# Loading the front of a fused state-space and MLP kernel in fewer, longer transfers

## The chip, the core and the metric

The kernel runs on one core of one Trainium2 chip. The metric is the device time of one execution in microseconds (us), as the median of several executions. Five engines run their own instruction lists in order and wait for each other through semaphores: PE (matrix multiply), DVE (vector), ACT (scalar functions), POOL (general) and SP, which in this kernel does nothing but issue DMA transfers between memory (HBM) and the on-chip buffer (SBUF), or from one place of SBUF to another.

## What is computed

The sequence has S = 2048 rows and D = 512 channels, in bf16. Part A is a state-space mixer, part B a sequence-mixing MLP; both sit on a residual stream.

```
def _A_ref(q, k, v, shift_k, ssm_k, ssm_D):      # q is layernormed
    k_shift = sum over t<4 of k_pad[:, t:t+S] * shift_k[:, 3-t]
    kv = k_shift * v
    y = causal convolution of kv with ssm_k, by FFT of length 2*S
    y = y + kv * ssm_D
    return q * y
def _B_ref(x, w1, w2, w3, w4):
    h = _gelu(_layernorm(x) @ w1)                # then shifts by 1 or 2 rows per quarter
    x1 = x + hs                                  # hs = shifted h @ w2
    return x1 + _gelu(_layernorm(x1) @ w3) @ w4
x = A_q
h = x + _A_ref(_layernorm(x), A_k, A_v, A_shift_k, A_ssm_k, A_ssm_D)
out = h + _B_ref(_layernorm(h), B_w1, B_w2, B_w3, B_w4)
```

## The kernel before, in words

Row s of the sequence is written s = 32 n + 16 h + t, with n < 64, h < 2 and t < 16. The long convolution is a Fourier transform of 64 x 32 points, done as matrix products.

**The order is written out by hand.** The function does not issue instructions directly. Every step is registered with `add` (lines 87 to 105) as a numbered operation with the engines that may do it, a planned cost, what it reads and what it writes. `plan.issue()` then walks the text `ISSUE` (lines 40 to 72): a list of operation numbers, each with a letter (A, V, G) where the engine is a choice. So each engine's program is the order of this list. The planned costs decide nothing at run time.

**Transfers.** All of them go out from SP, in the order of the list, through `dma` (line 218). In the front they are these. `load_k`, `load_v`, `load_h` (lines 221 to 231) bring k, v and the long filter `ssm_k` in twelve transfers of 512 KB, each to all 128 partitions. Line 233 brings the 512 x 4 taps of the short filter into `ssk_bf` in pieces of 8 bytes, line 239 the 512 values of `ssm_D` into `dcol` in pieces of 2 bytes. `k_rows` (lines 426 to 433) moves the product kv from its row layout (`kvqt`, two buffers) to the layout that the transform wants (`Rk`): 16 transfers of 128 KB, each from every second partition and for 256 of the 512 channels, in pieces of 512 bytes. Lines 511 to 514 load the first EARLY = 8 of the 16 rows per partition of q into the place of k once k has been read (two transfers of 512 KB, each to 64 partitions). Lines 366 to 371 spread a table into `Wc` in four transfers. Lines 547 to 549 load all of q into `q_sb`, as two transfers of 1 MB to 64 partitions each, and lines 532 to 539 move four pieces of a second table (`Wf2`).

```
        for h in range(2):
            for g in range(2):
                dma(0.5, lambda h=h, g=g: nc.sync.dma_start(
                    Rk()[g * N1:(g + 1) * N1, 16 * h + 4 * qr:16 * h + 4 * qr + 4, :],
                    kvqt[qr % 2][h:P:2, :, g * 256:(g + 1) * 256]),
```

**The compute of the front.** `k_transposed` (line 383) turns k on PE, four rows at a time (`pk`), and ACT copies the result to `kta`. `k_taps` (line 406) applies the short filter as 32 products per half group with the diagonal matrices `dg` (`psh`, line 417) and DVE multiplies by v into `kvq` (line 422). `dg` is built by DVE at line 299 from the identity matrix and the taps. `h_layout` (line 436) turns the long filter on PE after POOL has added `ssm_D` to its first column (line 517). Stage A (`stage_a`, line 453) is 32 groups of products, 16 of k (`pak`) and 16 of the filter (`pah`); ACT or DVE converts each into `Tk` or `Th` (lines 161 and 163). `Th` lies where the tables lay that `Wc` is filled from, so its conversions wait for those transfers. Stage C (`stage_c`, line 478) multiplies `Th` and `Tk` with `Wc` (`pch`, `pck`), the results are converted to `xt`, and `product` (line 601) multiplies the two spectra on DVE (lines 616 to 623). The mean and variance of every row of q are taken on DVE (`stats`, line 575, operations `bst` at line 576 and `mvq` at line 577): rows 0 to 7 from the early copy, rows 8 to 15 from `q_sb`. These have their places in DVE's list too, among the conversions and products. After that follow the inverse transform, the gate with normalized q, and part B, which keeps PE busy to the end.

Of the kernel before, what the change touches and what calls it, by code (L numbers as in the profile page):

```python
# [16 lines left out]
P = 128  # L17
# [23 lines left out]
23 2 20 4 0 8 1 3 5 21 6 33 10 37 7 13 27 24 12 28 25 9 82 11 30 18 83A 17 92 69 43 26 80 120 93A 14 15 31G 22  # L41
102 32 94 81A 41 71G 96 72 58 42 95 45 103A 86 97 127 46V 59 84 63 61 121 60 47 100 64 98 130 36 87 19 101 53G
99 62 112 54 16 44 85 55 56 122 131A 39 89 123 219 91 40 213 88 90 223 34 128 124A 220 207 35 209 38 104 224 57
211 129A 29 113 49 67 65 125 225 66 48 68 70 50G 105 114 203 126A 210 51 212 73G 106 214 221 52 115 183 132 226
74 119 179 107 75 177 76 111 185 78 170 184A 180V 110 117 178A 199 77 116 186V 175 108 200A 193 118 176V 197
194A 109 191 204 192V 198A 205 173 195 174A 208 79 189 206 196V 154 190A 156 155V 142 157A 152 222 153V 166 229
143A 217 164 215 227 228 165V 167A 140 138 141V 139A 171 181 172A 182V 144 187 145A 188V 201 150 202A 256 160
151V 146 161A 168 147V 162 169A 148 249 158 163A 263 255 159V 149A 261 237 264A 257 243 259 133 262A 258V 134
271 260A 137 273 135 245 272A 136 269 265 274A 275 266 270A 281 244 268 276A 287 267 285 282A 246 278 283 288A
277 284A 299 279 297 286A 280 300A 293 290 295 298A 289 311 296A 216 294V 305 312A 307 218 291 306A 309 292 302  # L50
321 310A 323 301 308A 317 322A 303 304 324A 329 313 319 318A 314 331 320A 333 315 330A 316 335 250 334A 325 345
332A 326 336A 343 328 341 346A 327 247 347 418 342A 337 383 361 364 338 344A 363 231 365 348A 340 362 339 349
350 352 351 248 353 388 354 398 389A 355 356 386 399A 358 396 357 387A 390 366 360 359 397A 394 391V 368G 404
395A 369G 405V 406 384 407A 367G 385V 392 414 251 393A 253 230 415V 408 252 400 409A 372G 402 401V 410 403A 412
371G 411V 419 413A 373G 235 374A 416 460 254 381V 379G 233 468 461A 238 236 234 232 469A 462 420 463 370A 428
470 421A 466 417 471 500 239 464 240 472 429A 241 474 242 501A 508 422 473 475 376A 467 465 430 377A 423 548 431
375A 424 476 378A 477 426 509A 478 434 479 432 484A 540 427 502 485A 488 694 435 510 486A 433 489 425 511 487A
503 380A 491 436 512 438 549A 437 504 490 514 439 446A 447V 382G 505 506 444A 450 515 513 507 445A 516 492 518
451V 517 541A 519 448 524V 525A 542 528 498 449A 527V 550 529 493 454 543 499 520 546 458 455 531 551 526A 496
521 547 554 459 530 452 544 497 480 481 456 552 453 545 494 553 555 457 482 556 558 532 557 495 536 533 559 565V  # L60
589 564V 537 569 483 566V 567V 560 570 534 440 590 522 441 538 591 568 596 442 586 539 443 598 571 535 597 599
612 587 588 592 572 593 584 578 573 594 523 576 595 579 614 600 602 601 574 613 577 615 575 603 604V 607A 605V
606V 608 616 638 609A 617 580 624 610 641 581 611V 640 713 618 585 717 714 582 583 701 620 561 718 646 695 702
562 639 563 697 619 625 643 703 698 642 696 667 622 704 623 648 719 621 668 626 627 699 647 720 644 705 649 645
700 650 715 651 706 652 653 711 716 628 709 712 629 632V 707 654 710 655 660V 721 708 669 661 630A 664 636V 722
633 656A 724 666 634A 657 665 658V 637 674 670 671 662V 728 663 672 659 673 676 729 680 675 723 631 677 725 635
684 682 683 678 726 679 685 775 730 757 776 766 732 791 758 727 747 681 792 692V 690A 733 748 745 734 759 746
686A 739 760 687 737 740 735 738 691 741 736 753 693 742 755 754 731 749 756 751 750 743 752 793 744 789 794 783
790 785 767 771 768 762 772 804 688A 786 689 761 784 770 769 811 763 795 812 765 787 796 781 788 779 782 773 780
797 774 777 798 835 778 823 836 821 813 805 814 822 824 817 806 819 818 799 807 829 820 808 842 809 764 830 831  # L70
810 825 832 815 826 827 833 800 834 828 816 838 801 802 837 803 847 839 840 841 843 848 849 850 844 846 845
# [50 lines left out]
def kernel(  # L122
# [48 lines left out]
    FUSED = ()  # L171
    EARLY = (8)
# [4 lines left out]
    slot("B", [P, 15360], "kta")  # L177
# [17 lines left out]
    def dg():  # L195
        return X["kta"][:, 9216:11264].rearrange("p (c j s) -> p c j s", c=DC, s=P)
# [16 lines left out]
    dcol = cst.tile([P, DC], BF16)  # L213
    ssk_bf = cst.tile([P, DC, 4], BF16)
# [6 lines left out]
    def load_k(r0):  # L221
        dma(1.4, lambda: nc.sync.dma_start(k_sb()[:, r0:r0 + 4, :], kd.rearrange("(p t) d -> p t d", t=NT)[:, r0:r0 + 4, :]),
            r=("C",), w=[("k", r) for r in range(r0, r0 + 4)])

    def load_v(qr):
        dma(1.4, lambda: nc.sync.dma_start(v_sb()[:, qr, :, :], vd[:, 4 * qr:4 * qr + 4, :]),
            r=("C",), w=[("v", qr)])

    def load_h(c):
        dma(1.4, lambda: nc.sync.dma_start(X["hraw"][:, c, :], A_ssm_k[c * P:(c + 1) * P, :]),  # L230
            r=("S1",), w=[("h", c)])

    dma(0.5, lambda: nc.sync.dma_start(ssk_bf[:], A_shift_k.rearrange("(c p) j -> p c j", p=P)), w=["sskb"])
# [5 lines left out]
    dma(0.5, lambda: nc.sync.dma_start(dcol[:], A_ssm_D.rearrange("(c p) -> p c", p=P)), w=["dcol"])  # L239
# [38 lines left out]
    add({"G": 0.6}, lambda: make_identity(nc, ident[:]), w=["id"])  # L278

# [6 lines left out]
    def numbers():  # L286
# [11 lines left out]
    add({"V": 1.1}, numbers, r=["pidx"], w=["pf"])  # L298
    v(2.3, lambda: V.tensor_tensor(
        out=dg().rearrange("p c j s -> p (c j) s"), in0=ident[:].unsqueeze(1).to_broadcast([P, 4 * DC, P]),  # L300
        in1=ssk_bf[:].rearrange("p c j -> p (c j)").unsqueeze(2).to_broadcast([P, 4 * DC, P]), op=MUL),
# [64 lines left out]
    for d in range(4):  # L366
        dma(1.5, lambda d=d: nc.sync.dma_start(
            X["Wc"][d:P:4, :, :, d].rearrange("p a b c d -> p (a b) (c d)"),
            X["tta"][d:P:4, 0:6144].rearrange("p (a x) -> p a x", a=48)),
            r=["A", "W"] + [("t", a, hf) for a in range(3) for hf in range(2)] + [("wz", a, e) for a in range(3) for e in range(4)],  # L370
            w=[("Wc", d)])
# [32 lines left out]
    kvqt = [cst.tile([P, 4, D], BF16, name=f"kvq{i}") for i in range(2)]  # L404

    def k_taps(qr, u):
# [3 lines left out]
        def pe():  # L410
            pv = psum("psb", key)[:].rearrange("p (t d) -> p t d", d=D)
            for i in range(2):
                for c in range(DC):
                    for j in range(4):
# [3 lines left out]
                                  rhs=dg()[:, c, j, :], start=(j == 0), stop=(j == 3))  # L418
# [4 lines left out]
            out=kvqt[qr % 2][:, 2 * u:2 * u + 2, :], in0=X[key][:].rearrange("p (t d) -> p t d", d=D),  # L423
            in1=v_sb()[:, qr, 2 * u:2 * u + 2, :], op=MUL), ["C", key, ("v", qr)], [("kvq", qr % 2, u)])

    def k_rows(qr):

        for h in range(2):
            for g in range(2):
                dma(0.5, lambda h=h, g=g: nc.sync.dma_start(  # L430
                    Rk()[g * N1:(g + 1) * N1, 16 * h + 4 * qr:16 * h + 4 * qr + 4, :],
                    kvqt[qr % 2][h:P:2, :, g * 256:(g + 1) * 256]),
                    r=["C", ("kvq", qr % 2, 0), ("kvq", qr % 2, 1)], w=[("Rk", qr, h, g)])
# [19 lines left out]
    def stage_a(w, i, ring):  # L453
# [14 lines left out]
        if w == "k":  # L468
            src = ["C"] + [("Rk", qr, h, g) for qr in range(4) for h in range(2) for g in range(2)]
        else:  # L470
            src = ["S2"] + [("Rh", cc, b) for cc in range(2) for b in range(2)]
# [6 lines left out]
    def stage_c(w, c, hf, ring):  # L478
# [17 lines left out]
        add({"A": 1.05, "V": 1.4},  # L496
# [13 lines left out]
    qd = A_q[0].rearrange("(n h t) d -> h n t d", h=2, t=NT)  # L510
    for h in range(2 if EARLY else 0):
        dma(0.3 * EARLY, lambda h=h: nc.sync.dma_start(
            k_sb()[h * N1:(h + 1) * N1, 0:EARLY, :], qd[h, :, 0:EARLY, :]),
            r=("C",), w=[("k", t) for t in range(EARLY)])

    for cc in range(2):
        add({"G": 0.3}, lambda cc=cc: G.tensor_tensor(out=X["hraw"][:, cc:DC:2, 0], in0=X["hraw"][:, cc:DC:2, 0],
                                                      in1=dcol[:, cc:DC:2], op=ADD),
            ["S1", "dcol"], [("h", cc), ("h", cc + 2)])
# [12 lines left out]
    for hf in range(2):  # L532
        for h in range(2):
# [4 lines left out]
            dma(0.4, rows, wfs + [("kvq", 1, 0), ("kvq", 1, 1)],  # L538
# [9 lines left out]
    for h in range(2):  # L548
        dma(4.0, lambda h=h: nc.sync.dma_start(X["q_sb"][h * N1:(h + 1) * N1, :, :], qd[h]), r=["S1"], w=[("q", h)])
# [11 lines left out]
    def power(r, var, n, rk, wk):  # L561
        pool(0.33 + 0.165 * n, lambda: G.tensor_tensor(out=r, in0=var, in1=half[:, 0:n], op=OP.pow), ["half", rk], [wk])
# [16 lines left out]
    def q_stats(t0):  # L579
        for t in range(t0, t0 + 4):  # L580
            if t < EARLY:
                stats(lambda t: k_sb()[:, t, :], mvq, t, ["C", ("k", t)], "mvq")
            else:
                stats(lambda t: X["q_sb"][:, t, :], mvq, t, ["S1", ("q", 0), ("q", 1)], "mvq")
# [377 lines left out]
```

## Time and profile before

| what | value |
|---|---|
| median of 3 runs | 262.74 us (261.31 to 264.78) |
| the profiled execution's own time | 264.27 us |
| its span, first to last instruction | 262.4 us |
| busy in the span: PE, DVE, ACT, POOL | 220.8, 161.1, 147.4, 60.5 us |
| moved by DMA | 23.91 MB |
| mean granted clock of PE | 0.933 |

The page gives one line for each engine with its busy share in 40 slices of 6.56 us, as tenths, and below them the DMA engines' share and rate. The chain that ended last names, step by step, what the next step waited for. A group line names the source line, the engine, what is written from what, and how often. Durations and starts are those of one execution, and its own time is 1.5 us over the median of the runs.

### The profile page before, as it was taken

The numbers are of one execution on the slowest core, as the hardware profiler recorded it, in microseconds if no ns is written. First come the engines' busy times: TensorE is split into PE (matmuls) and PEld (weight loads), VectorE is DVE, ScalarE is ACT, GpSimd is POOL, SyncE is SP. The second block draws the span as 40 slices with busy tenths as digits, with TensorE's granted clock in tenths as the row PEclk, the third lists the DMA queues.
The fourth block names the chain that finished last, engine by engine and source line by source line (L and its number), as shares of the span: only waits on it lengthen the run. The fifth ranks groups of instructions, "written<-read, shape, count | busy, mean of one in ns | idle before, by whom it ended". The sixth has DMA issues, their size and how long they took to land.

```text
span 262.4 us, 4615 instructions
## 1 busy us (share of the span) xinstructions
PE 220.8 (84%) x1874; PEld 142.8 (54%) x1886; DVE 161.1 (61%) x287; ACT 147.4 (56%) x185; POOL 60.5 (23%) x110
## 2 busy tenths in 40 slices
PE   2697685588999948764399999999999999999993
PEld 2697685467999948632144454444444444444441
DVE  5866268779999999999883879567400141050321
ACT  1695372779998976999874345550475036334000
POOL 9923640031000003833765040404000000000000
PEclk9999799559999995999579999999999999999999
DMA  6899999995100039700324100054220020010021
GB/s 175 307 250 232 216 176 203 168 213 112 42 2 1 2 93 381 249 2 1 80 60 81 23 0 0 0 82 84 56 61 23 0 60 21 2 45 15 22 59 41
DMA packets 31894, 23.91 MB, mean 91 GB/s; under 512 B 21248, under 2 KB 28416, under 8 KB 31616
## 3 DMA queue, kind: packets, MB, share of 16 engines
q1 hardware_dynamic: 31872, 23.61, 38.6%
q8 instruction: 15, 0.25, 0.4%
q14 instruction: 7, 0.06, 0.1%
HBM read 14.16 MB, written 2.10 MB: 62 GB/s over the span
## 4 chain that ended last, share of the span: by engine, by line
PE 56%; DVE 19%; DMA 15%; SPq 3%; ACT 3%; issue 2%; POOL 1%; DVEq 0%; ACTq 0%
PE pw L792 24%; PE p L919 18%; DMA kin<-in_A_q_dram 7%; PE p L858 5%; DMA kin<-kvq 5%; DVE Yp L616 5%; DMA dcol<-in_A_ssm_D_dram 4%; DVE Tk L163 3%; DVE bst L576 3%; PE pg L674 2%; SPq L430 2%; DVE hh L741 1%; DVE Gs L163 1%; DVE kvq L422 1%; DVE Yp L623 1%
## 5 line engine op out<-in xcount | busy, mean ns | idle before, releaser
L792 PE MATMUL pw<-act,wts 128*128 128x512 bf16 x283 | 65.3, 387 | 1.2 <-issue 1.0
L796 ACT ACTIVATE g<-pw 128x512 bf16<-128x512 f32 x56 | 32.5, 596 | 50.2 <-PE pw L792 48.2
L919 PE MATMUL p<-wts,g 128*128 128x512 bf16 x220 | 49.0, 379 | 0.3
L792 PEld LDWEIGHTS <-wts 128*128 128x128 bf16 x288 | 28.5, 99 | 35.8 <-issue 3.2
L924 DVE TENSOR_TENSOR wts<-p,wts 128x1024 bf16<-128x1024 f32 (+1 forms) x9 | 10.0, 1106 | 60.6 <-PE p L919 60.6
L919 PEld LDWEIGHTS <-g 128*128 128x128 bf16 x224 | 21.9, 98 | 26.5
L576 DVE BATCH_NORM_STATS2 bst<-hh 128x6 f32<-128x512 bf16 x32 | 20.7, 678 | 0.0
L616 DVE TENSOR_TENSOR Yp<-xt 128x2048 bf16<-128x2048 bf16 (+1 forms) x20 | 19.3, 1008 | 0.9 <-ACT xt L161 0.6
L417 PE MATMUL psh<-kta 128*128 128x128 bf16 x256 | 15.2, 220 | 2.2 <-DVE kvq L422 2.2
L161 ACT CAST xt<-pch 128x1024 bf16<-128x1024 f32 x16 | 16.1, 1047 | 0.7 <-PE pch L491 0.7
L662 POOL TENSOR_SCALAR qn<-q_sb,rq,vq 128x512 bf16<-128x512 bf16 x8 | 6.4, 807 | 43.1 <-ACT Gs L161 43.0
L864 DVE SCALAR_TENSOR_TENSOR hh<-hh,rho,p 128x512 bf16<-128x512 bf16 x16 | 11.3, 741 | 8.0 <-PE p L858 4.8
L417 PEld LDWEIGHTS <-kta 128*128 128x128 bf16 x256 | 14.5, 98 | 2.6 <-issue 2.3
L488 PE MATMUL pck<-Tk,Wc 128*128 128x256 bf16 x64 | 14.6, 273 | 1.0 <-ACT xt L161 1.0
L490 PEld LDWEIGHTS <-Wc 128*128 128x128 bf16 x128 | 14.5, 113 | 1.3 <-issue 1.3
L161 ACT CAST xt<-pck 128x1024 bf16<-128x1024 f32 x14 | 14.1, 1028 | 1.8 <-PE pck L491 1.8
L858 PE MATMUL p<-wts,act 128*128 128x512 bf16 x61 | 14.8, 380 | 0.2
L488 PE MATMUL pch<-Th,Wc 128*128 128x256 bf16 x64 | 14.6, 273 | 0.0
L488 PEld LDWEIGHTS <-Wc 128*128 128x128 bf16 x128 | 14.5, 113 | 0.1
L491 PEld LDWEIGHTS <-Wc 128*128 128x128 bf16 x128 | 14.5, 113 | 0.0
L796 ACT ACTIVATE act<-pw 128x512 bf16<-128x512 f32 x16 | 9.4, 596 | 9.0 <-PE pw L792 9.0
L674 PE MATMUL pg<-CSG,Yp 128*128 128x128 bf16 x128 | 10.3, 254 | 4.6 <-DVE Yp L620 4.3
(129 smaller groups left out, 403.6 us busy)
## 6 DMA issues: line engine op xcount, KB each, us to landing
wts<-in_B_w_dram SPq DMA_DIRECT2D x2, 1792.0 KB, 10.6
kin<-in_A_k_dram SPq DMA_DIRECT2D x4, 512.0 KB, 7.7
kin<-in_A_v_dram SPq DMA_DIRECT2D x4, 512.0 KB, 10.9
hraw<-in_A_ssm_k_dram SPq DMA_DIRECT2D x4, 512.0 KB, 14.2
kin<-kvq SPq DMA_DIRECT2D x16, 128.0 KB, 6.3
q_sb<-in_A_q_dram SPq DMA_DIRECT2D x2, 1024.0 KB, 11.9
out_dram<-wts SPq DMA_DIRECT2D x14, 128.0 KB, 2.3
Wc<-tta SPq DMA_DIRECT2D x4, 384.0 KB, 7.1
```

The costliest lines, as they stand in the source:

```text
L161: A.copy(o, src)
L417: T_.matmul(pv[:, i, c * P:(c + 1) * P], lhsT=kT()[:, c, r % NT, s0:s0 + P], rhs=dg()[:, c, j, :], start=(j == 0), stop=(j == 3))
L488: T_.matmul(pv[:, kk, :, :].rearrange("p r d -> p (r d)"), lhsT=W[0], rhs=Tw.rearrange("p r d -> p (r d)"), start=True, stop=False)
L490: T_.matmul(pv[:, kk, 0, :], lhsT=W[1], rhs=Tw[:, 1, :], start=False, stop=False)
L491: T_.matmul(pv[:, kk, 1, :], lhsT=W[2], rhs=Tw[:, 0, :], start=False, stop=True)
L576: v(0.68, lambda: V.bn_stats(bst[:, t, :], x(t)), r, [("bst", t)], lat=0.08)
L616: v(0.08 + 1.14 * s, lambda i=i: V.tensor_tensor(out=pr(i), in0=x(0), in1=x(1)[:, i:i + 1].to_broadcast([P, 2, n, 8]), op=MUL), ["C"] + rx ...
L674: T_.matmul(pv[:, ee, :], lhsT=X["Yp"][:, (8 * i + ee) * P:(8 * i + ee + 1) * P], rhs=CSG[:], start=True, stop=True)
L792: T_.matmul(ps[:], lhsT=wt(w)[:, k, m * P:(m + 1) * P], rhs=xT()[:, k, 4 * b * P:(4 * b + 4) * P], start=(k == 0), stop=(k == DC - 1))
L796: add({"A": 0.59}, lambda: A.activation(dst(), X[pkey][:], ACT.Gelu_apprx_tanh), r + [pkey, "gelu"], [key])
L858: T_.matmul(ps[:, i, :], lhsT=gT()[:, m, t + i + 2 + off[m], :], rhs=wt("w2")[:, m, :], start=(m == 0), stop=(m == 3))
L919: T_.matmul(ps[:, i, :], lhsT=X["g2"][:, b % 2, m, s0:s0 + P], rhs=wt("w4")[:, m, :], start=(m == 0), stop=(m == FC - 1))
```

## The change

The change has five parts (1 to 5) and a new list (6).

1. `kvqt` is laid out by channel halves, and `k_rows` issues two transfers of 256 KB for each group of four rows instead of four of 128 KB, in pieces of 2 KB instead of 512 bytes. DVE's product at line 422 writes the new layout.
2. q is loaded with a source pattern written by hand (`all_rows`), so that one transfer fills all 128 partitions: one of 1 MB for the early half and one of 2 MB for all of it, in place of two each.
3. The short filter and `ssm_D` are loaded as rows (four partitions of 1 KB and four of 256 bytes) and turned into columns on PE (`columns`, five transposes) with one copy to `ssk_bf`. `dcol` goes, and `dg` has its taps outermost.
4. PE multiplies a block of zeros 32 times at the start (`busy`).
5. Slot B grows by 1,024 columns to hold the rows and the zeros, and some planned costs are new numbers.
6. `ISSUE` is another list. The first loads go in the order k0, k4, k12, k8, v3, v1, v0, h1, h3, then early q, v2, h2, h0. The identity is made as POOL's sixth operation instead of its first. The first row statistics that read `q_sb` stand on DVE before two of stage A's conversions, and all eight of them before the first spectral product; in the list before, four of them came after it.

```diff
-23 2 20 4 0 8 1 3 5 21 6 33 10 37 7 13 27 24 12 28 25 9 82 11 30 18 83A 17 92 69 43 26 80 120 93A 14 15 31G 22
...
+2 31 3 20 4 0 1 5 7 33 34 21 24 22 6 25 9 26 40 11 8 23 27 13 19 77V 28 57V 12 78 29V 58 30 10 86 17 87A 18 94
...
+    WARM = (32)
...
-    slot("B", [P, 15360], "kta")
+    slot("B", [P, 16384], "kta")
...
-    dma(0.5, lambda: nc.sync.dma_start(ssk_bf[:], A_shift_k.rearrange("(c p) j -> p c j", p=P)), w=["sskb"])
+    dma(0.1, lambda: nc.sync.dma_start(rows5()[:, 0:4 * P], A_shift_k.rearrange("(c p) j -> c (p j)", p=P)), r=["B"], w=[("r5", 0)])
+    dma(0.1, lambda: nc.sync.dma_start(rows5()[:, 4 * P:], A_ssm_D.rearrange("(c p) -> c p", p=P)), r=["B"], w=[("r5", 1)])
...
-    dma(0.5, lambda: nc.sync.dma_start(dcol[:], A_ssm_D.rearrange("(c p) -> p c", p=P)), w=["dcol"])
...
+    def busy():
+
+        pv = psum("psb", ("p0",))
+        for i in range(WARM):
+            T_.matmul(pv[:, 0:P], lhsT=zero(), rhs=zero(), start=True, stop=True)
...
+    def columns():
+        pt = psum("psa", ("p5",), True)
+        for j in range(5):
+            T_.transpose(pt[:, DC * j:DC * j + DC], rows5()[:, j:4 * P:4] if j < 4 else rows5()[:, 4 * P:], ident[0:DC, 0:DC])
...
-    kvqt = [cst.tile([P, 4, D], BF16, name=f"kvq{i}") for i in range(2)]
+    kvqt = [cst.tile([P, 2, 4 * 256], BF16, name=f"kvq{i}") for i in range(2)]
...
-        for h in range(2):
-            for g in range(2):
-                dma(0.5, lambda h=h, g=g: nc.sync.dma_start(
-                    Rk()[g * N1:(g + 1) * N1, 16 * h + 4 * qr:16 * h + 4 * qr + 4, :],
-                    kvqt[qr % 2][h:P:2, :, g * 256:(g + 1) * 256]),
-                    r=["C", ("kvq", qr % 2, 0), ("kvq", qr % 2, 1)], w=[("Rk", qr, h, g)])
+        for g in range(2):
+            dma(1.0, lambda g=g: nc.sync.dma_start(
+                Rk()[g * N1:(g + 1) * N1].rearrange("p (h r) d -> p h r d", h=2)[:, :, 4 * qr:4 * qr + 4, :],
+                kvqt[qr % 2][:, g, :].rearrange("p (t d) -> p t d", d=256)),
+                r=["C", ("kvq", qr % 2, 0), ("kvq", qr % 2, 1)], w=[("Rk", qr, g)])
...
-    qd = A_q[0].rearrange("(n h t) d -> h n t d", h=2, t=NT)
-    for h in range(2 if EARLY else 0):
-        dma(0.3 * EARLY, lambda h=h: nc.sync.dma_start(
-            k_sb()[h * N1:(h + 1) * N1, 0:EARLY, :], qd[h, :, 0:EARLY, :]),
+    def all_rows(t0, t1):
+
+        return bass.AP(A_q[0].tensor, A_q[0].offset + t0 * D, [[NT * D, 2], [N2 * D, N1], [1, (t1 - t0) * D]])
+
+    if EARLY:
+        dma(0.33 * EARLY, lambda: nc.sync.dma_start(k_sb()[:, 0:EARLY, :], all_rows(0, EARLY)),
             r=("C",), w=[("k", t) for t in range(EARLY)])
...
-    for h in range(2):
-        dma(4.0, lambda h=h: nc.sync.dma_start(X["q_sb"][h * N1:(h + 1) * N1, :, :], qd[h]), r=["S1"], w=[("q", h)])
+    dma(5.3, lambda: nc.sync.dma_start(X["q_sb"][:], all_rows(0, NT)), r=["S1"], w=["q"])
```

The pattern in `all_rows` is a list of pairs of step and count, outermost first: 2 blocks (h) that lie 16 rows apart, within each 64 rows of blocks (n) that lie 32 rows apart, and then the contiguous elements of 8 or 16 rows. In the kernel before, the two blocks were two transfers, each with the count 64 outermost.

More of the change, by code (lines that the diff above doesn't have):

```diff
@@ L46 @@
[L46 to L55, printed above, removed]
@@ L210, in um, with rows5, zero @@
         return umt
-    dcol = cst.tile([P, DC], BF16)
-    ssk_bf = cst.tile([P, DC, 4], BF16)
+    def rows5():
+        return X["kta"][0:DC, 15360:16000]
+    def zero():
+        return X["kta"][:, 16000:16128]
+    ssk_bf = cst.tile([P, 5, DC], BF16)
     kd = A_k[0]
@@ L278 @@
     add({"G": 0.6}, lambda: make_identity(nc, ident[:]), w=["id"])
+    v(0.1, lambda: V.memset(zero(), 0.0), ["B"], ["zero"])
+    def busy():
+        pv = psum("psb", ("p0",))
+        for i in range(WARM):
+            T_.matmul(pv[:, 0:P], lhsT=zero(), rhs=zero(), start=True, stop=True)
+    if WARM:
+        add({"P": 0.058 * WARM}, busy, ["B", "zero"], [("p0",)], opens=("psb", ("p0",)))
     def iotas():
@@ L298 @@
     add({"V": 1.1}, numbers, r=["pidx"], w=["pf"])
+    def columns():
+        pt = psum("psa", ("p5",), True)
+        for j in range(5):
+            T_.transpose(pt[:, DC * j:DC * j + DC], rows5()[:, j:4 * P:4] if j < 4 else rows5()[:, 4 * P:], ident[0:DC, 0:DC])
+    add({"P": 0.3}, columns, ["id", "B", ("r5", 0), ("r5", 1)], [("p5",)], opens=("psa", ("p5",)))
+    add({"A": 0.25, "V": 0.12}, lambda e: evac(e, ssk_bf[:].rearrange("p j c -> p (j c)"), X[("p5",)][:, 0:5 * DC]),
+        [("p5",)], ["sskb"])
     v(2.3, lambda: V.tensor_tensor(
-        out=dg().rearrange("p c j s -> p (c j) s"), in0=ident[:].unsqueeze(1).to_broadcast([P, 4 * DC, P]),
-        in1=ssk_bf[:].rearrange("p c j -> p (c j)").unsqueeze(2).to_broadcast([P, 4 * DC, P]), op=MUL),
+        out=dg().rearrange("p j c s -> p (j c) s"), in0=ident[:].unsqueeze(1).to_broadcast([P, 4 * DC, P]),
+        in1=ssk_bf[:, 0:4, :].rearrange("p j c -> p (j c)").unsqueeze(2).to_broadcast([P, 4 * DC, P]), op=MUL),
       ["id", "sskb", "B"], ["dg"])
@@ L366 @@
     for d in range(4):
-        dma(1.5, lambda d=d: nc.sync.dma_start(
+        dma(1.75, lambda d=d: nc.sync.dma_start(
             X["Wc"][d:P:4, :, :, d].rearrange("p a b c d -> p (a b) (c d)"),
@@ L417, in pe @@
                         T_.matmul(pv[:, i, c * P:(c + 1) * P], lhsT=kT()[:, c, r % NT, s0:s0 + P],
-                                  rhs=dg()[:, c, j, :], start=(j == 0), stop=(j == 3))
+                                  rhs=dg()[:, j, c, :], start=(j == 0), stop=(j == 3))
         add(mm(32), pe, ["B"] + [("kT", (t0 + j) % NT) for j in range(-3, 2)] +
@@ L422, in k_taps @@
         v(1.23, lambda: V.tensor_tensor(
-            out=kvqt[qr % 2][:, 2 * u:2 * u + 2, :], in0=X[key][:].rearrange("p (t d) -> p t d", d=D),
-            in1=v_sb()[:, qr, 2 * u:2 * u + 2, :], op=MUL), ["C", key, ("v", qr)], [("kvq", qr % 2, u)])
+            out=kvqt[qr % 2][:].rearrange("p g (t d) -> p t g d", d=256)[:, 2 * u:2 * u + 2],
+            in0=X[key][:].rearrange("p (t g d) -> p t g d", g=2, d=256),
+            in1=v_sb()[:, qr, 2 * u:2 * u + 2, :].rearrange("p t (g d) -> p t g d", g=2), op=MUL), ["C", key, ("v", qr)], [("kvq", qr % 2, u)])
     def k_rows(qr):
-        for h in range(2):
-            for g in range(2):
-                dma(0.5, lambda h=h, g=g: nc.sync.dma_start(
-                    Rk()[g * N1:(g + 1) * N1, 16 * h + 4 * qr:16 * h + 4 * qr + 4, :],
-                    kvqt[qr % 2][h:P:2, :, g * 256:(g + 1) * 256]),
-                    r=["C", ("kvq", qr % 2, 0), ("kvq", qr % 2, 1)], w=[("Rk", qr, h, g)])
+        for g in range(2):
[3 more added lines that the diff above has]
+                r=["C", ("kvq", qr % 2, 0), ("kvq", qr % 2, 1)], w=[("Rk", qr, g)])
     def h_layout(cc, b):
@@ L468, in stage_a @@
         if w == "k":
-            src = ["C"] + [("Rk", qr, h, g) for qr in range(4) for h in range(2) for g in range(2)]
+            src = ["C"] + [("Rk", qr, g) for qr in range(4) for g in range(2)]
         else:
@@ L495, in stage_c @@
         wi = 0 if w == "k" else 1
-        add({"A": 1.05, "V": 1.4},
+        add({"A": 1.05, "V": 1.23},
             lambda e: evac(e, X["xt"][:, wi, c % 2, :, :, 4 * hf:4 * hf + 4],
@@ L517 @@
         add({"G": 0.3}, lambda cc=cc: G.tensor_tensor(out=X["hraw"][:, cc:DC:2, 0], in0=X["hraw"][:, cc:DC:2, 0],
-                                                      in1=dcol[:, cc:DC:2], op=ADD),
-            ["S1", "dcol"], [("h", cc), ("h", cc + 2)])
+                                                      in1=ssk_bf[:, 4, cc:DC:2], op=ADD),
+            ["S1", "sskb"], [("h", cc), ("h", cc + 2)])
         for b in range(2):
@@ L537, in rows @@
                 nc.sync.dma_start(flat2(kvqt[0][:])[64 * h:64 * h + 64, x], src[64 - 64 * h:128 - 64 * h, x])
-            dma(0.4, rows, wfs + [("kvq", 1, 0), ("kvq", 1, 1)],
+            dma(0.6, rows, wfs + [("kvq", 1, 0), ("kvq", 1, 1)],
                 [("Wf", 1, hf, h)] + ([("kvq", 0, 0), ("kvq", 0, 1)] if (hf, h) == (0, 0) else []))
@@ L561, in power @@
     def power(r, var, n, rk, wk):
-        pool(0.33 + 0.165 * n, lambda: G.tensor_tensor(out=r, in0=var, in1=half[:, 0:n], op=OP.pow), ["half", rk], [wk])
+        pool(0.3 + 0.18 * n, lambda: G.tensor_tensor(out=r, in0=var, in1=half[:, 0:n], op=OP.pow), ["half", rk], [wk])
     def root(mv, var, r, nm, n, rk, key, add2=None):
@@ L583, in q_stats @@
             else:
-                stats(lambda t: X["q_sb"][:, t, :], mvq, t, ["S1", ("q", 0), ("q", 1)], "mvq")
+                stats(lambda t: X["q_sb"][:, t, :], mvq, t, ["S1", "q"], "mvq")
         x = slice(t0, t0 + 4)
@@ L663, in qnorm @@
                                 op0=MUL, op1=ADD)
-        add({"A": 0.81, "V": 0.41, "G": 1.06}, qnorm, ["S1", "S2", ("q", 0), ("q", 1), ("rq", t - t % 4, "r"), ("rq", t - t % 4, "m")], [("qn", t)])
+        add({"A": 0.81, "V": 0.41, "G": 0.83}, qnorm, ["S1", "S2", "q", ("rq", t - t % 4, "r"), ("rq", t - t % 4, "m")], [("qn", t)])
     slot("A", [P, N2, 2, 4, 64], "Gs")
```

55 lines of the change are left out of this document (31 added, 24 removed), and 3 rows, old and new, of the table ISSUE.

## The prediction

> **What bounds the kernel now.** I read the page's slices first, then the chain that ended last, the waits of SP and the tiles, and last the windows and DVE's timeline.
>
> ```profile
> DMA  6899999995100039700324100054220020010021
> GB/s 175 307 250 232 216 176 203 168 213 112 42 2 1 2 93 381 249 2 1 80 60 81 23 0 0 0 82 84 56 61 23 0 60 21 2 45 15 22 59 41
> ...
> q1 hardware_dynamic: 31872, 23.61, 38.6%
> ```
>
> The DMA engines are nine tenths busy up to 59 us while the rate falls to 168 to 250 GB/s, against 381 when the weights are loaded. So the front is bound by transfers that go slowly. The chain says which:
>
> ```profile
> 3.14 9.62 DMA dcol<-in_A_ssm_D_dram
> 12.77 18.22 DMA kin<-in_A_q_dram
> 31.01 0.59 SPq L430
> ...
> 32.30 6.85 DMA kin<-kvq
> ...
> 48.72 5.70 DMA kin<-kvq
> ```
>
> Start, duration, what: SP could issue the second early q only when dcol had landed, and a kvq transfer only when that q had. In SP's order each of these waits is for the transfer eight before it. So at most eight are in flight, and one slow transfer stops those behind it.
>
> ```profile
> 15.00:17.00 2.00, 2.00 (x39) 2.00 (x37) 1.16 (x1) 2.00 (x3) 0.00 (x0) 1.00 1.12 219
> 98.00:99.00 1.00, 0.00 (x0) 0.00 (x0) 0.97 (x3) 0.00 (x0) 0.00 (x0) 0.50 1.03 423
> 99.00:100.00 1.00, 0.74 (x8) 0.74 (x9) 1.00 (x4) 0.00 (x0) 0.00 (x0) 0.50 1.00 409
> 100.00:101.00 1.00, 1.00 (x12) 1.00 (x11) 0.97 (x3) 0.67 (x1) 0.00 (x0) 0.50 1.05 430
> ```
>
> The last column is GB/s. Early q runs in the first window, weights in the others. Their mean is 421 GB/s, 26.3 for each of the 16 DMA engines.
>
> ```profile
> 64.39 0.67 DVE L576 BATCH_NORM_STATS2 bst<-q_sb 128x6 f32<-128x512 bf16 x1
> ...
> 69.83 2.36 DVE L616 TENSOR_TENSOR Yp<-xt 128x2048 bf16<-128x2048 bf16 x2
> ...
> 65.00:78.00 13.00, 12.69 (x172) 12.57 (x170) 12.34 (x18) 11.86 (x14) 0.00 (x0) 1.00 0.10 23
> 78.00:100.00 22.00, 17.01 (x224) 16.64 (x224) 21.54 (x31) 17.68 (x19) 0.00 (x0) 0.94 0.17 59
> ```
>
> The third busy number is DVE's: from 65 to 100 us it is full. Whatever delays DVE's arrival at the first spectral product (69.83) delays the end by as much. DVE first reads q_sb at 64.39 and does not wait for it now. I take this point as the measure of the change.
>
> **Part by part.**
>
> *Small inputs.* Before: pieces of 8 and 2 bytes, dcol landing after 9.6 us. After: eight pieces. Five transposes (4 columns each, at most the 0.118 us of a pk transpose) and a copy of 0.12 to 0.25 us replace them. The identity moves behind POOL's umt iotas (0.19 and 0.15), the tta iota (3.17), pidx (0.27) and a memset (0.95), so it is there at 4 to 6 us instead of 1.3. The first k lands about then (PE starts on it at 5.19), so this costs 0 to 0.8 us, under cover of later loads. DVE's dg (2.29 us, start 7.90) keeps its place or comes 1 us sooner.
>
> *Zeros.* 32 matmuls at 0.109 to 0.118 us (the first pk transposes took 1.89 us for 16, the next 3.48 for 32, the last 1.05 for 16) are 3.6 us, ending about when k lands. PE waits 7.0 us for k in this stretch. At most 48 x 0.045 = 2.2 us of PE comes back, none on the path: 0. If k came sooner than the zeros end, they would cost up to 1 us.
>
> *kvq rows.* 16 issues at 0.61 us become 8: SP saves 4.9 us, of which 2.5 lie in the last group (43 to 49 us). In the last landing (5.70 us), 0 to 3 us can go. Writing by halves leaves DVE's product at 1.22 us: same elements, runs of 256. Taken alone: 2.5 to 5.5 us.
>
> *q in one transfer.* No row shows this pattern, and it decides. Its source has the count 2 outermost. In the trace every one of the 88 transfers has an outer count that 16 divides (32, 64, 128), and every one has 16 landing records: each is dealt out in 16 equal shares of its outer loop. An outer loop of 2 has only two equal shares. Upper price: the two engines alone move it at 26.3 GB/s each, 524 KB each for early q = 19.9 us, 1,049 KB each for q = 39.9 us. Lower price: all 16 share it at 421 GB/s, 2.5 and 5.0 us. I take the two engines, because the shares in the trace go by the outer loop without an exception. At the rate of the 15 to 17 window (13.7 GB/s an engine) it would be 38 and 77 us, but there half of the partitions took all 16 engines' writes, and here each engine has a half to itself, so the 26.3 is nearer.
>
> [...]
>
> **The sum**, as the load on one of the two engines (its sixteenth of everything else, its half of q):
> - the nine loads ahead of early q, 4.72 MB: 11.2 us at 421 GB/s, 17.6 at 268 (mean of the 2 us windows from 2 to 12 us, 216 to 334); 14 taken, starting at 2: 16 us
> - early q: 19.9, to 36
> - v2, h2, h0: 98 KB at 26.3: 3.7, to 40. Loads of h0 and v2 thus come some 13 us later than now (POOL's second add at 28.34 waited for h0)
> - kvq rows, 131 KB: 5 to 12 us (26.3, or 10.8 as in 43 to 49 us); 7, and Wc: 7.1 from issue to landing; 7: to 54. The last rows can be issued only after DVE's kvq, which waits for the eight early statistics (8 x 0.68, behind early q), for h0's transposes (2.0 each) and for the rows two groups earlier: 54. SP's eight-back rule makes Wc wait for early q too, 36; it is not later for that
> - q: 39.9, and 3 for gaps and the landing: 97.
>
> At 97 DVE stands at the first statistic on q_sb, with stage A's Th 11 and Tk 8 behind it, so stage C cannot start. Then 8 x 0.68 + 8 x 0.09 + 2 conversions x 1.22 + 2 xt x 1.22 = 11, and 1.5 for PE (its stage C starts only after Th 11 and, after 30 us of idling, at the half clock that 49 to 57 us showed): the product starts at 109.5 instead of 69.83, 39.7 later. Four statistics that came after that point are done by then: minus 2.7. So plus 37. The savings above (rows, small inputs) end in waits for q. 264.27 + 37 = 301 for the profiled execution; the median lies 1.5 below it: **300**.
>
> **Rivals.**
>
> *q runs on all 16 engines: faster.* Then early q gains 4.8 - 2.5 = 2.3 us against the 219 GB/s window, small inputs up to 3 (2 to 12 us at 421 instead of 268 would save 3.6), the last rows 2.5 of issue and about 2 of landing: 10 us in all, 264.3 - 10 less the 1.5 = **253**. For it: the weights' 421 GB/s with 128 partitions. Against: their outer count is 128. It decides from four engines up: 3.15 MB of q take 60 us on two engines, 30 on four, which puts the arrival at 67, where DVE gets to it now.
>
> *The transfers are hidden.* q on 16 engines, but stage A's 32 conversions (1.03 on ACT, 1.22 on DVE, 17.7 us from 47.4 to 65.1) start no earlier than Wc and the kvq chain allow: only issue and landing count, 2.5 + 2: **258**. For it: ACT and DVE already fill 52 to 65 us (11.1 and 11.6 of 13).
>
> *Two engines, but at the slower rate* (13.7): q arrives 18 + 37 us later, 355. Against it stands the lack of crowding named above; between the two, 20 GB/s gives 320.
>
> **How the numbers follow.** About 2% is what a measurement of this kernel can tell from no change: 257.5 to 268. Two engines 0.83, nearly all slower by over 2%; all engines and 253: 0.12, of which 0.02 would end within 2%; hidden, 258: 0.05, half of it within 2%. So slower 0.83, same 0.04, faster 0.13. The likeliest gives 300. Its low end: 28.7 GB/s an engine (459 in the window 14.5 to 15) takes 5 us off, and no gaps and fast rows 8 more: 287. Its high end lies toward the slow rate, 340. That leaves out the 0.17 of the other cases and about 0.03 above, so the range is the likeliest case's own, 287 to 340.
>
> **What would show it.** Right: early q landing some 20 to 30 us after issue and q over 40; GB/s near 50 in the slices from 60 to 95 us; DVE idle for 25 to 40 us ahead of a bst on q_sb, released by the q transfer; fewer than 16 landing records for q; the kvq rows issued in half the time. Wrong: q landing within 3 to 8 us of issue, or a product that starts before 70 us; then the order and the rows carry the result.

## The result and the profile after

The changed kernel takes 310.31 us (median of 4 runs, 309.05 to 310.94) beside 262.84 us of the kernel before (261.31 to 264.78): a ratio of 1.180, with a 95% interval of 1.171 to 1.189. The profiled execution took 309.69 us, its span is 307.9 us and the mean granted clock 0.871.

First the page of the kernel after, DMA share and rate in 40 slices (now 7.7 us each):

```profile
DMA  6974415763111100005910324000250310110032
GB/s 205 417 216 93 94 61 152 136 109 92 51 55 53 50 3 2 3 0 172 378 68 1 68 36 86 16 0 2 52 114 7 69 34 0 37 34 0 2 75 61
```

The rate falls to 61 to 94 GB/s in slices 4 to 6 (23 to 46 us) and stands at 50 to 55 from 77 to 108 us. The windows of the kernel after follow. Behind each stretch and its length stand the busy time of PE, PE's weight loads, DVE, ACT and POOL (with the number of instructions), PE's granted clock, the DMA engines' share and GB/s:

```profile
35.00:44.00 9.00, 0.00 (x0) 0.00 (x0) 0.00 (x0) 0.00 (x0) 0.00 (x0) 0.50 0.24 69
...
80.00:90.00 10.00, 0.00 (x0) 0.00 (x0) 0.00 (x0) 0.00 (x0) 0.00 (x0) 0.50 0.13 54
90.00:100.00 10.00, 0.00 (x0) 0.00 (x0) 0.00 (x0) 0.00 (x0) 0.00 (x0) 0.50 0.13 54
117.00:130.00 13.00, 12.56 (x171) 12.45 (x169) 12.74 (x18) 12.35 (x14) 4.71 (x4) 1.00 0.01 3
```

A share of 0.13 is two engines of sixteen, and 54 GB/s are 27 for each. No compute engine does anything from 35 to 44 us and from 80 to 100 us. DVE's timeline of the kernel after says what it waits for (start, duration, what, and in brackets the idle time before it with its releaser; `kin` is the place of k, into which early q goes):

```profile
44.49 1.88 DVE L602 BATCH_NORM_STATS2 bst<-kin 128x6 f32<-128x512 bf16 x3 [21.93 <-DMA kin<-in_A_q_dram]
...
107.24 0.69 DVE L602 BATCH_NORM_STATS2 bst<-q_sb 128x6 f32<-128x512 bf16 x1 [31.86 <-DMA q_sb<-in_A_q_dram]
...
117.34 2.36 DVE L642 TENSOR_TENSOR Yp<-xt 128x2048 bf16<-128x2048 bf16 x2
```

The two waits for q are 53.8 us together. The first spectral product starts at 117.34 instead of 69.83, 47.5 later, and the span is 45.5 longer. The likely cause of the difference of 2.0 is the four statistics that now lie ahead of the product instead of behind it (2.7 was predicted). SP's timeline of the kernel after shows the queue of transfers (start, time from the first issue to the end of the last, waits between them included, count):

```profile
9.73 0.68 SPq L540 DMA_DIRECT2D kin<-in_A_q_dram  x1
...
16.05 19.48 SPq L455 DMA_DIRECT2D kin<-kvq  x4
44.47 9.12 SPq L392 DMA_DIRECT2D Wc<-tta  x4
55.55 6.79 SPq L455 DMA_DIRECT2D kin<-kvq  x4
62.45 0.57 SPq L575 DMA_DIRECT2D q_sb<-in_A_q_dram  x1
```

Early q was issued at 9.73 and its last landing is recorded at 44.4. The first Wc transfer, the eighth after it, was issued at that moment. q went out at 62.45 and landed at 107.2. In the trace's records each of the two q transfers has 3 landing records, one at the issue and two at the end (10.82, 42.47 and 44.40 us for early q; 63.57, 106.80 and 107.21 for q). In the kernel before all 88 transfers have 16. So with the count 2 outermost there are two landings, beside a share of two engines. The two small inputs of the kernel after, whose rows have a count of 4 outermost, have four landings and one record at the issue. What the record at the issue stands for, no run shows.

### The profile page after: what moved, and what is told of

Read it like the earlier page. It is cut to its first block, busy times and chain, and to the rows that moved or that the text cites. A ratio compares the mean times of both kernels' runs of the same rounds, so it can differ in the third digit from the quotient of the medians.

```text
span 307.9 us, 4674 instructions
## 1 busy us (share of the span) xinstructions
PE 224.4 (73%) x1911; PEld 146.5 (48%) x1923; DVE 162.0 (53%) x297; ACT 137.5 (45%) x174; POOL 68.0 (22%) x112
## 5 line engine op out<-in xcount | busy, mean ns | idle before, releaser
L945 PEld LDWEIGHTS <-g 128*128 128x128 bf16 x224 | 21.9, 98 | 26.5
L489 PE MATMUL pak<-WA,kin 64*128 64x128 bf16 x128 | 8.8, 281 | 34.3 <-DVE Th L163 31.8
L161 ACT CAST Tk<-pak 128x1024 bf16<-128x1024 f32 x12 | 11.7, 1030 | 34.1 <-PE pak L489 32.2
L470 PE MATMUL pt<-ident,hraw 128*64 128x128 bf16 x128 | 7.8, 288 | 23.9 <-POOL hraw L544 23.9
L489 PEld LDWEIGHTS <-kin 64*128 64x128 bf16 x128 | 7.7, 188 | 35.7 <-issue 35.6
L602 DVE BATCH_NORM_STATS2 bst<-q_sb 128x6 f32<-128x512 bf16 x8 | 5.1, 678 | 31.9 <-DMA q_sb<-in_A_q_dram 31.9
L161 ACT COPY Rh<-pt 128x2048 bf16<-128x2048 bf16 x4 | 7.4, 1865 | 30.7 <-PE pt L470 30.7
L470 PEld LDWEIGHTS <-hraw 128*64 128x64 bf16 x128 | 7.4, 205 | 24.3 <-POOL hraw L544 24.0
L442 PE MATMUL psh<-kta 128*128 128x128 bf16 x256 | 16.8, 231 | 0.0
L602 DVE BATCH_NORM_STATS2 bst<-kin 128x6 f32<-128x512 bf16 x8 | 5.1, 679 | 21.9 <-DMA kin<-in_A_q_dram 21.9
L442 PEld LDWEIGHTS <-kta 128*128 128x128 bf16 x256 | 15.9, 104 | 0.4 <-DVE kta L163 0.2
L884 PE MATMUL p<-wts,act 128*128 128x512 bf16 x63 | 14.9, 380 | 0.1
## 6 DMA issues: line engine op xcount, KB each, us to landing
hraw<-in_A_ssm_k_dram SPq DMA_DIRECT2D x4, 512.0 KB, 35.3
kin<-kvq SPq DMA_DIRECT2D x8, 256.0 KB, 12.5
```

The lines of the kernel that those rows point to most:

```text
L161: A.copy(o, src)
L442: T_.matmul(pv[:, i, c * P:(c + 1) * P], lhsT=kT()[:, c, r % NT, s0:s0 + P], rhs=dg()[:, j, c, :], start=(j == 0), stop=(j == 3))
L470: T_.transpose(ptv[g * N1:(g + 1) * N1, n, :], X["hraw"][:, 2 * g + cc, n2:S:N2], ident[:])
L489: T_.matmul(pv[:, g, ee, :], lhsT=Rf[g * N1:(g + 1) * N1, e:N2 * 256:64], rhs=WA[g * N1:(g + 1) * N1, :, :].rearrange("p a b -> p (a b)"), ...
L602: v(0.68, lambda: V.bn_stats(bst[:, t, :], x(t)), r, [("bst", t)], lat=0.08)
L884: T_.matmul(ps[:, i, :], lhsT=gT()[:, m, t + i + 2 + off[m], :], rhs=wt("w2")[:, m, :], start=(m == 0), stop=(m == 3))
```

## The experiments

The theory: the count 2 outermost in q's source confines each q transfer to two engines, and that is the whole loss. One rival: the new list, the zeros or the longer rows cost time of their own. A second: the transfers are as quick as before, but one transfer makes rows wait that each half released sooner. The landings above already speak against this one: q took 44.8 us from issue to landing, where its two halves took 14.5 together before. All ratios are to the kernel before on the same chip; its medians were 266.46, 264.32 and 266.15 us in three sets of runs.

**Each q load in halves again.** Both, the early one alone, the late one alone; all else as in the kernel after. (The comments in this and the next pieces of code name the runs.)

```diff
-        dma(0.33 * EARLY, lambda: nc.sync.dma_start(k_sb()[:, 0:EARLY, :], all_rows(0, EARLY)),
+            for h in range(2):                                       # q_halves, early_halves
+                nc.sync.dma_start(k_sb()[h * N1:(h + 1) * N1, 0:EARLY, :], qd[h, :, 0:EARLY, :])
...
-    dma(5.3, lambda: nc.sync.dma_start(X["q_sb"][:], all_rows(0, NT)), r=["S1"], w=["q"])
+        for h in range(2):                                           # q_halves, late_halves
+            nc.sync.dma_start(X["q_sb"][h * N1:(h + 1) * N1, :, :], qh[h])
```

> The changed kernel, with both loads of q issued again as two transfers of 64 partitions each (count 64 outermost); everything else as changed. Theory (the outer count of 2 puts q on two engines, and all of the loss comes from that): no wait of DVE for q over 3 us, product start near 61 us, 250 to 258 us. Rival (the new list or the rows in halves cost the time): the wait for early q shrinks but the time stays over 285 us. Second rival (the transfers are hidden anyway): 258 to 264 us.

Measured: 263.94 us, ratio 0.990 (0.983 to 0.998). The loss is gone, and all the rest of the change together brings 1%, less than expected. DVE's wait for q is 2.75 us, as the theory has it, but the product starts at 72.07 and not near 61; the time lies in the range of the second rival. What holds it there is followed up below.

> The changed kernel with only early q as two transfers of 64 partitions; the 2 MB load stays one transfer. Theory: early q lands by 25 us, the 2 MB load is issued near 42 us instead of 62 and still takes 40 us and a few, so DVE gets it at 84 to 90 us; the product starts at 95 to 100 us, 288 to 294 us in all. Rival (early q alone is the cause, the 2 MB load is slow only because it stands behind it): 255 to 265 us.

Measured: 290.29 us, ratio 1.091 (1.082 to 1.099).

> The changed kernel with only the 2 MB load of q as two transfers of 64 partitions; early q stays one transfer. Theory: DVE's wait of 31.9 us for the 2 MB load goes, that of 21.9 us for early q stays; the product starts at 85 to 88 us, 277 to 282 us in all. Rival (the 2 MB load is what counts, early q is hidden): 255 to 262 us.

Measured: 281.01 us, ratio 1.056 (1.048 to 1.064). From 310.3 the early part is worth 20.0, the late one 29.3, both 46.4: nearly a sum (310.3 is from another set of runs, in which the kernel before took 262.84). DVE's timeline of early_halves and then of late_halves:

```profile
86.84 0.69 DVE L607 BATCH_NORM_STATS2 bst<-q_sb 128x6 f32<-128x512 bf16 x1 [30.72 <-DMA q_sb<-in_A_q_dram]
...
98.07 2.36 DVE L647 TENSOR_TENSOR Yp<-xt 128x2048 bf16<-128x2048 bf16 x2
```

```profile
44.57 1.88 DVE L607 BATCH_NORM_STATS2 bst<-kin 128x6 f32<-128x512 bf16 x3 [21.95 <-DMA kin<-in_A_q_dram]
...
79.16 0.70 DVE L607 BATCH_NORM_STATS2 bst<-q_sb 128x6 f32<-128x512 bf16 x1 [3.38 <-DMA q_sb<-in_A_q_dram]
```

Each part leaves the wait of the other in place: 30.7 us for q, or 21.95 for early q. In late_halves a wait of 3.38 for q is left, and the product starts at 89.26, a little later than expected.

**The same pattern in the kernel before.** One part alone, in the old list.

```diff
-            k_sb()[h * N1:(h + 1) * N1, 0:EARLY, :], qd[h, :, 0:EARLY, :]),
+            k_sb()[:, 0:EARLY, :], all_rows(0, EARLY))) if h == 0 else (lambda: None),     # before_one_early
...
-        dma(4.0, lambda h=h: nc.sync.dma_start(X["q_sb"][h * N1:(h + 1) * N1, :, :], qd[h]), r=["S1"], w=[("q", h)])
+        dma(4.0, (lambda: nc.sync.dma_start(X["q_sb"][:], all_rows(0, NT))) if h == 0 else (lambda: None),   # before_one_late
```

> The kernel before, in its own order, with one thing changed: early q as one transfer with the count 2 outermost. Theory (two engines, and every later transfer has a share behind it): early q lands near 40 us instead of 31, DVE waits for it 9 us or more longer, and the end moves by 8 to 17 us: 274 to 284 us. Rival (the loss needs the new order too): within 4 us of before.

Measured: 275.61 us, ratio 1.045 (1.034 to 1.056). DVE's wait for early q ends at 40.42 instead of 31.08.

> The kernel before with one thing changed: the 2 MB load of q as one transfer with the count 2 outermost. Theory: issued at 49 us it lands at 92 to 95 us; DVE, which now reads it at 64 us, stands until then; 290 to 298 us. Rival (in the old order the statistics stand late enough to hide it): within 4 us of before.

Measured: 295.34 us, ratio 1.120 (1.108 to 1.132). DVE's timeline of before_one_late:

```profile
95.96 0.69 DVE L580 BATCH_NORM_STATS2 bst<-q_sb 128x6 f32<-128x512 bf16 x1 [29.34 <-DMA q_sb<-in_A_q_dram]
```

So the pattern costs its time without the new list, the zeros or the rows, and the first rival does not explain that. One transfer of q with a large count outermost was not tried.

**The place of the statistics.** In stats_late the kernel after is kept and only the list changed: all eight statistics on `q_sb` and their roots stand behind the spectral products.

> The changed kernel with nothing but its list edited: the row statistics that read the 2 MB load of q, and POOL's roots of them, stand behind all spectral products instead of before two of stage A's conversions. Theory (the 2 MB load costs only because DVE stops in its list for it): the same transfer still lands near 107 us, but DVE goes on; 276 to 283 us. Rival (the slow transfer harms through the queue behind it, tables and rows): over 295 us.

Measured: 285.18 us, ratio 1.071 (1.063 to 1.080). DVE's timeline of stats_late:

```profile
84.92 2.36 DVE L641 TENSOR_TENSOR Yp<-xt 128x2048 bf16<-128x2048 bf16 x2 [0.71 <-ACT xt L160]
```

The product starts 32.4 us sooner, the time falls by 25. The late statistics now stand, from 118.6 to 123.5, in front of conversions that PE waits for (5.0 us), so some of it is given back; the range was missed by a little. It shows that the 2 MB transfer itself is slow but need not be waited for at that point.

**Where the rest's gain went.** SP's timeline of q_halves:

```profile
15.88 6.14 SPq L455 DMA_DIRECT2D kin<-kvq  x4
24.55 12.14 SPq L392 DMA_DIRECT2D Wc<-tta  x4
36.97 7.47 SPq L455 DMA_DIRECT2D kin<-kvq  x4
```

and its DVE and PE timelines:

```profile
59.89 0.69 DVE L612 BATCH_NORM_STATS2 bst<-q_sb 128x6 f32<-128x512 bf16 x1 [2.75 <-DMA q_sb<-in_A_q_dram]
...
72.07 2.36 DVE L652 TENSOR_TENSOR Yp<-xt 128x2048 bf16<-128x2048 bf16 x2
```

```profile
63.19 0.37 PE L513 MATMUL pch<-Th,Wc 128*128 128x256 bf16 x1 [1.59 <-ACT Tk L161]
...
63.57 0.42 PE L513 MATMUL pch<-Th,Wc 128*128 128x256 bf16 x1
```

The conversions of stage A begin at 43.2 instead of 47.5, but DVE then waits 2.75 for q, stage A's last conversions stand behind that, and PE comes out of the pause at half clock (0.50 from 60 to 66 us; 0.42 us for a product that takes 0.27 at full clock). The product ends up 2.2 later than before. halves_mid is q_halves with one number of the list moved: the first statistic that reads `q_sb` (241) goes behind the two conversions.

```diff
-137 193A 180 216 181V 186 221 138A 223 147 222 187V 148A 172 212 178 224 173A 179V 161 163 162A 188 241 149 250
...
+138A 223 147 222 187V 148A 172 212 178 224 173A 179V 161 163 162A 188 149 250 189V 164A 141 142A 139 150V 159 140A 241
```

> The kernel with both loads of q in halves, and the one row statistic that stops DVE for 2.8 us moved behind the two stage A conversions that stand after it. Theory (those conversions are what PE's stage C waits for): stage C starts 2 to 3 us sooner, 260 to 262 us against 264. Rival (the half clock of PE at that point limits it): no change, 263 to 265 us.

Measured: 259.47 us, ratio 0.985 (0.977 to 0.992), a little better than expected. Its PE and DVE timelines:

```profile
60.30 0.28 PE L512 MATMUL pch<-Th,Wc 128*128 128x256 bf16 x1 [0.62 <-DMA q_sb<-in_A_q_dram]
```

```profile
66.91 2.34 DVE L651 TENSOR_TENSOR Yp<-xt 128x2048 bf16<-128x2048 bf16 x2
```

Stage C starts 2.9 us sooner and at full clock (1.00 from 60 to 66 us), the product 5.2 sooner.

In two_queues, q_halves again, the second half of each q load is issued by ACT, so that the halves run side by side.

```diff
-            nc.sync.dma_start(X["q_sb"][h * N1:(h + 1) * N1, :, :], qh[h])
+            (nc.sync, nc.scalar)[h].dma_start(X["q_sb"][h * N1:(h + 1) * N1, :, :], qh[h])
```

> The kernel with both loads of q in halves, but the second half of each is issued by ACT, so that the two halves are in flight side by side. Theory (a transfer to 64 partitions is slow because all 16 engines write to one half of the partitions): the 2 MB load lands 6 to 9 us after its issue instead of some 15 and early q 2 to 4 us sooner, DVE's wait of 2.8 us goes: 258 to 262 us. Rival (halves are as fast one after the other): 263 to 266 us, landings unchanged.

Measured: 264.41 us (260.4 to 265.86) beside 264.32 of the kernel before (261.83 to 266.68). The runs spread too widely to tell a change, and the landings decide: the halves of q land 15.0 and 15.9 us after their issue, against 9.3 and 14.7 in q_halves, and a 16 KB piece takes 1,293 ns (median) in both. The theory that side by side is faster falls.

**Which part carries the gain.** Four kernels built on halves_mid: the rows in four transfers a group again, one zero product instead of 32, the small inputs as columns again (at the head of SP's list, with one small copy on DVE), and all three together. Then the list is what is new; beside it stay one product of zeros, the small copy, the order of the taps in `dg` and the larger slot.

```diff
-    kvqt = [cst.tile([P, 2, 4 * 256], BF16, name=f"kvq{i}") for i in range(2)]
+    kvqt = [cst.tile([P, 4, D], BF16, name=f"kvq{i}") for i in range(2)]            # mid_rows4, mid_list, with the old k_rows
...
-    WARM = (32)
+    WARM = (1)                                                                      # mid_zero1, mid_list
...
-    dma(0.1, lambda: nc.sync.dma_start(rows5()[:, 0:4 * P], A_shift_k.rearrange("(c p) j -> c (p j)", p=P)), r=["B"], w=[("r5", 0)])
+    dma(0.1, lambda: nc.sync.dma_start(ssk_raw[:], A_shift_k.rearrange("(c p) j -> p c j", p=P)), r=["B"], w=[("r5", 0)])   # mid_small, mid_list
```

> The kernel of halves_mid with part 1 undone: kvqt in rows again, four transfers of 128 KB for each group (issued as two pairs). halves_mid took 259.5 us beside 263.5 of the kernel before. Theory: the fewer rows transfers are what the change gains, since stage A's conversions started 4.2 us sooner in q_halves than before; then this one takes 262 to 264. Rival: the longer pieces are paid back in the issues of the Wc and kvq transfers that hold SP (12.1 us for Wc against 7.7 before), then 258.5 to 261.

Measured: 258.82 us, ratio 0.972 (0.967 to 0.976). The theory falls.

> halves_mid with one product of zeros at the start instead of 32. Theory: the zeros bring nothing and cost nothing, 258.5 to 260.5. Rival: they keep PE at full clock when k lands, and without them k's transposes end later and the whole front with them by 1 to 2 us, 260.5 to 262.

Measured: 258.01 us, ratio 0.970 (0.964 to 0.976). The zeros bring nothing that can be told.

> halves_mid with the small inputs loaded as columns again (pieces of 8 and 2 bytes, at the head of SP's list), one small copy on DVE in place of PE's five transposes. Theory: the many small pieces slow the loads behind them at the start and dg comes later, 0.5 to 3 us, so 260 to 262.5. Rival: both are under the wait for k and v, 258.5 to 260.

Measured: 258.93 us, ratio 0.973 (0.967 to 0.978). The theory falls: as columns at the head of the list they cost nothing that can be told.

> halves_mid with the rows transfers, the zeros and the small inputs all undone, so that only the new list (with the one statistic moved) stands against the kernel before. Theory: the sum of the three single runs, 263 to 266, no faster than the kernel before. Rival: the list is the gain, 258 to 261.

Measured: 257.24 us (256.1 to 257.8), ratio 0.965 (0.960 to 0.970). The theory falls and its rival holds: the list is the gain, and the three parts bring nothing beside it. This version is faster than the kernel before and the one after. halves_mid ran in another set, at 259.47 us, so it is not told apart from the four within some 2 us. Within their set all six runs of mid_list lie under all six of mid_rows4 (258.52 to 259.01), so the zeros and the new small inputs cost 1.6 us there rather than gain. DVE's timeline of the kernel before (first line) and of mid_list:

```profile
31.08 1.88 DVE L576 BATCH_NORM_STATS2 bst<-kin 128x6 f32<-128x512 bf16 x3 [6.95 <-DMA kin<-in_A_q_dram]
```

```profile
23.09 1.86 DVE L614 BATCH_NORM_STATS2 bst<-kin 128x6 f32<-128x512 bf16 x3
...
57.61 3.65 DVE L614 BATCH_NORM_STATS2 bst<-q_sb 128x6 f32<-128x512 bf16 x6
...
64.69 2.34 DVE L654 TENSOR_TENSOR Yp<-xt 128x2048 bf16<-128x2048 bf16 x2
```

DVE's wait for early q (6.95 us) is gone. The product starts 5.1 us sooner than before, with no wait for q, and the four statistics ahead of it (2.7) add up with that to 7.8 of the 8.1 us by which the span is shorter (254.3 against 262.4). The windows of the kernel before and of mid_list show where it begins:

```profile
5.00:10.00 5.00, 3.01 (x27) 2.75 (x28) 4.97 (x6) 1.86 (x1) 4.79 (x3) 1.00 0.86 268
10.00:15.00 5.00, 4.63 (x65) 4.51 (x63) 2.59 (x3) 4.17 (x4) 4.53 (x5) 1.00 0.99 383
```

```profile
5.00:10.00 5.00, 3.59 (x32) 3.44 (x33) 4.41 (x11) 1.92 (x2) 4.92 (x8) 1.00 1.00 379
10.00:15.00 5.00, 5.00 (x75) 5.00 (x75) 4.90 (x5) 2.14 (x5) 1.33 (x2) 1.00 1.03 419
```

The same loads run at 379 instead of 268 GB/s. dcol, which in the kernel before was issued behind four loads of k, landed after 9.6 us and released early q, is the first transfer here and lands after 2.7. The traces of all eleven kernels with the new list or a variant of it have 361 to 388 GB/s from 5 to 10 us, with the small inputs as rows or as columns, and the three with the old list 257 to 268. That the faster start is what the list gains, rather than another of its moves, is argued from these traces; no run moved the first loads alone.

Why do longer pieces of kv not help? mid_list and halves_mid have the same list. In the trace's records a 512-byte piece of kv takes 44.5 ns in the mean in mid_list, and a 2 KB piece 183.5 ns in halves_mid: 11.5 and 11.2 GB/s an engine. All pieces together take 182 us of engine time, summed over the 16 engines, in the one and 188 in the other (205 in the kernel before). The rows of DMA issues (count, size, us from issue to landing) of halves_mid and then of mid_list:

```profile
kin<-kvq SPq DMA_DIRECT2D x8, 256.0 KB, 9.1
```

```profile
kin<-kvq SPq DMA_DIRECT2D x16, 128.0 KB, 5.5
```

Half as many transfers, each twice the size, land after 9.1 instead of 5.5 us, and the bytes move no faster.

## Why the prediction was right, and by how much it missed

The outcome and the mechanism were right, the range held the time, and the forecast of 300 was 10 us short. Of the signs that were to show it two did not come: early q landed 34.7 us after its issue, not 20 to 30, and SP took 26.3 us for the rows' issues and the waits between them (19.48 and 6.79), where half of the 14.9 of before was forecast. Step by step:

- **q is dealt to two engines**: right. Two landings for each transfer, a share of 0.13, 54 GB/s in all where 52.6 was taken.
- **Ahead of early q, 16 us**: right. Its first pieces in the trace's records start at 15.1.
- **Early q, 19.9 us, landing at 36**: mis-sized. Its last piece ends at 43.9 and DVE goes on at 44.5, 8.5 later than forecast. An 8 KB piece takes 313 ns alone (26 GB/s, the price taken), but up to 1,093 while other transfers run. Over the 64 pieces that each of the two engines moves, this costs 2.0 us up to 21 us, where the last loads run (on these two engines as well or not, the records do not tell), and 5.9 in four later stretches, in which the first four transfers of kv rows run. The sum had the two engines' shares of the rows behind early q, and there they were: of each of these transfers 112 of 128 pieces, the shares of 14 engines, run in those stretches, and the last 16 only from 45 us on. What the sum left out is that these two slow down while the other engines move the rows. Why they do, no run shows.
- **v2, h2, h0, rows, Wc: 17.7, to 54**: the size was right (18.0 from 44.5 to q's issue at 62.45), the reason only in part. The two engines' shares of v2, h2 and h0 were done 3.9 us after early q (3.7 taken). But Wc waited for early q as the transfer eight before it, and then SP took 9.12 us for Wc's issues and 6.79 for those of the last rows, 4.3 of it one wait for DVE's kvq; it was not the two engines' load alone.
- **q, 39.9 and 3 for gaps: 97**: 44.8 from issue to landing. The first piece starts 3.1 after the issue, the pieces take 41.2, and 0.5 is left to the landing, so the term is 1.8 short.
- **From the landing to the product, 12.5**: 10.1 measured, 2.4 too much. The terms together: 8.5 + 1.8 - 2.4 = 7.9, and 109.5 + 7.9 is the 117.4 that the trace shows. The four statistics gave back 2.0 instead of 2.7, and the profiled execution is 8.4 us over its forecast of 301. The other 2 are the step to the median: it was taken to lie 1.5 below the profiled execution, as before, and it lies 0.6 above.
- **Zeros, 0**: right, as far as can be told (mid_zero1). **Small inputs**: right as an amount on the path, none (mid_small); the copy took 0.60 us on DVE, where the kernel's planned 0.12 to 0.25 were taken. The faster start that the first rival put down to them is there, but with their old form as well (379 GB/s in mid_list): it goes with the list.
- **Rows alone, 2.5 to 5.5 us**: mis-sized. SP's stretches for kv, waits included, take 13.6 us for 8 issues (q_halves) instead of 14.9 for 16, not 4.9 less, and the bytes move no faster (11.2 GB/s an engine in halves_mid, 11.5 in mid_list). Undoing them changes nothing that can be told (mid_rows4).
- **The rivals**: "all 16 engines", 253, is excluded by the landings, and with q in halves the rest of the change gives 263.9, not near 253. The 258 of "hidden" is met by halves_mid (259.5) and mid_list (257.2) only by chance: their gain comes from the list, which the prediction priced at nothing of its own. The slower rate, 355, is excluded: the pieces of q run at 26.7 GB/s an engine on two engines (median 614 ns for 16 KB).

## What to carry to other kernels

Before two transfers are merged into one, look at the outermost count of the new pattern: here a count of 2 in the source gave two landings, a DMA share of 0.13 and 54 GB/s, where every transfer with 32, 64 or 128 had 16 landings. What was queued behind such a transfer came late too: two of the 16 shares of v2, h2 and h0 landed at 43.7 to 48.3 us, the other 14 by 23.4. Price a longer piece by the measured time per byte of that kind of transfer (here 11.2 GB/s an engine in 2 KB pieces of kv against 11.5 in 512-byte pieces), not by its length, and look at the order before the shapes: here the new list was worth 3.5%, and the rows, zeros and small inputs beside it nothing.

## What the runs showed of the hardware that was not expected

- **SP was held inside an issue.** In the kernel after one issue of kv rows took 7.5 us (median 2.2, minimum 0.53), and in q_halves the four Wc issues took 12.1 against 7.7 before, with 2 KB rows ahead of them. In mid_list, with 512-byte rows ahead and the same list as halves_mid (12.35), they took 6.9. The 0.61 us that an issue of kv rows took before (median) is no price there.
- **Two shares of sixteen came late behind early q.** In the kernel after, 14 of the 16 shares of v2, h2 and h0 landed by 19.4, 21.9 and 23.4 us, the last two of each at 43.7 to 48.3, behind early q. The transfers h2 and h0 of the filter thus took 35.3 us each from issue to landing (before, median of its four: 14.2). POOL waited for them (us in all, times, longest wait):

```profile
POOL hraw L544 <- DMA hraw<-in_A_ssm_k_dram: 31.3, 2, 25.0
```

- **The transfers to 64 partitions moved at half the rate an engine.** A 16 KB piece of q takes 1,293 ns in halves on 16 engines (12.7 GB/s each, 203 in all), 614 ns on two engines, by the pattern one for each half (medians); the 4 KB pieces of k, v and the filter to 128 partitions take 159 ns (25.8 GB/s). The rows of kv, to 64 partitions too, go at 11.2 to 11.5. Why they go at half the rate, and why both halves at once on two queues stay at 1,293 ns, the runs leave open.
